# First dense pass of an attention, dense layer and routed expert kernel: work of the next block behind each step's own, five staging buffers, and expert tile 0 in another order

## The chip, the cores and the metric

The kernel runs on one core of one Trainium2 chip. The metric is the device time of one execution in microseconds (us). Before the change the median of three runs is 918.85 us (918.7 to 922.15).

## What is computed

```python
# 4 batches, 8 heads, 576 tokens, head size 64, 128 features
def phi(x):
    proj = np.einsum('bhsd,df->bhsf', x, w_phi)
    proj = proj - np.max(np.abs(proj), axis=-1, keepdims=True)
    return np.concatenate([np.exp(proj), np.exp(-proj)], axis=-1)
q_p, k_p = phi(q), phi(k)
kv, z = np.einsum('bhsf,bhsd->bhfd', k_p, v), np.sum(k_p, axis=2)
x = einsum('bhsf,bhfd->bhsd', q_p, kv) / (einsum('bhsf,bhf->bhs', q_p, z)[..., None] + 1e-06)
# x as 2304 tokens of 512
h = x @ w_in                                   # 512 x 2048
x = np.maximum(0.01 * h, h) @ w_out            # 2048 x 512
# cosine of each token to 8 expert embeddings over tau; the best expert and its softmax weight
for e in range(8):
    mask = expert_idx == e
    out[mask] = gate_w[mask, None] * (np.maximum(x[mask] @ w1[e], 0.0) @ w2[e])   # 512 x 1024 x 512
```

## The kernel before

**Tiling.** The 2304 tokens are nine blocks of 256 (`j`, 0 to 8). The attention works on four pairs of heads (`p`) and, for k and v, four batches (`b`). The dense layer's 2048 inner features are sixteen chunks (`c`); the first pass over the nine blocks uses chunks 0 to 7 and writes half sums `yp_d`, the second pass uses chunks 8 to 15, adds the half sums, and makes `ys`, the input of the router and the experts. In the second pass the blocks are worked through and the routing is done; then come the tiles of 128 gathered tokens of the experts. Expert tile 0 already begins before the last block's end.

Nearly every product of fp32 quality is made from two fp32r parts, hi and lo, as three fast matmuls (lines 344 to 346 of `mm1`, and 366 of `mm2`). Some projections of the attention are full fp32 matmuls instead, which need no split: of k where `b < K_FULL`, of q where the block is under `Q_FULL`.

**The attention.** For k, `k_load` fetches `kraw`, `k_split` makes hi and lo on ScalarE (ACT) and VectorE (DVE), `k1` projects on TensorE (PE), takes the largest absolute value and makes the two exponentials `kp`, `kn` (lines 180 and 181, ACT), `k2` multiplies with v into `kvp`, copied to `KV`. For q, `q_load` fetches `qraw`, `q1` projects (line 228 or 231), copies `pr` (line 234) and finds the largest value per token; for blocks under `QM_PE` that is done by transposing on PE (`qprT`, line 239), reducing on DVE (`qtm`, 241) and transposing back (`qmxT`, 247), for the others by a reduction over the partitions on GpSimd (POOL, line 252). `q2` subtracts it and makes the exponentials `qn`, `qp` (258, 259) and the products with `KV` (270) into `qo`; `q3` divides to `xr`, transposes it on PE (`xT`, 289) and makes `xb` hi (ACT, 293) and lo (DVE, 294), the dense layer's input. Pair `p` gives the part `k = p` of the sum over 512 in `mm1`, so the last pair is needed by every product.

**The weights.** `w_load(c)` converts two halves of 512 KB (`r`, 0 and 1) from float64: `w_fetch` issues the DMA on SyncE's queue (SP, line 307) into a staging buffer `wst` (three of them), ACT casts `top` (324), DVE puts the float together as `w` (328), ACT casts it to `W` hi (332), and POOL or, for the halves in `W_DVE`, DVE subtracts for `W` lo (333).

**The order.** The prelude (lines 430 to 448) does k of batch 0 and q of block 0, with `W0[p]` weight chunks after each pair. In block `j` each step `c` loads weights (block 0 only, up to chunk `c + W_AHEAD`), runs `mm1(j, c)`, then the step's items of the attention for block `j + 1` and of the next k batch, then `mm2(j, c - 2)`:

```python
            mm1(j, c, 200 if j == NBLK - 1 else 0)
            for it in steps[c]:
                it()
```

The order on each engine is set by the framework's scheduler, which simulates the program and puts each ready instruction by priority; `tc.issue_after(x)` keeps what is in it behind `x`. In the expert phase PE, and for the tiles in `I_ACT` ACT too, go in the order as written.

**The ends of the second pass.** `y_half_b(j)` is a generator in pieces: sums `ys` on DVE (602), a Square for the norm on ACT (605); then the eight dot products with the embeddings (613, DVE) for each half; then routing (631 onward). For blocks 7 and 8 the pieces are called from places in the expert tiles: `steps` (lines 1053 onward) maps a place (tile, position) to a piece; `ENDS` is (0, 1), `DOTS` (0, 2) and (1, 0). `first_split(3)` converts a quarter of the first expert's weights (ACT cast 900, DVE subtraction 901). In an expert tile, `up` multiplies (958 to 962) into `hps`, ACT makes `hs` (965), PE transposes it (`htp`, 972), ACT casts it to `h` hi (975), DVE subtracts for lo (976).

## Time and profile before

| what | value |
|---|---|
| median of three runs | 918.85 us (918.7 to 922.15) |
| profiled execution, its time | 917.62 us |
| span in the profile | 915.8 us |
| PE busy | 879.2 us (96%) |
| weight loads of PE busy | 754.8 us (82%) |
| DVE busy | 562.0 us (61%) |
| ACT busy | 448.8 us (49%) |
| POOL busy | 223.4 us (24%) |
| mean granted TensorE clock | 0.988 |

The span runs from the first to the last recorded instruction, and the execution's own time is 1.8 us more. A row of a timeline gives start, length, engine, line, operation, the tiles it writes and reads, and how many equal instructions it stands for; in brackets the idle time of the engine before it and what ended that. "x" counts instructions. A full fp32 matmul shows as two records, and a matmul's recorded length overlaps that of the next, so the pace is read from start to start. The clock is 1.00 where TensorE is granted its full 2.4 GHz.

### The profile page before, as it was taken

To read this page: it belongs to the slowest core of one execution; us is meant where nothing else is said; L and a number is where in the kernel's file an instruction comes from. 1 tells how busy PE (TensorE), PEld (TensorE's weight loads), DVE (VectorE), ACT (ScalarE), POOL (GpSimd) and SP (SyncE) were. 2 spreads that over 40 slices of the span, in tenths; PEclk is the share of its full clock that TensorE was granted. 3 is DMA by queue.
4 is the path that set the end of the run, shared out by engine and by line. 5 is a ranking of instruction groups with operands and counts; after the bars stand their busy time and mean duration, and the time that the engine had idled before them with its cause. 6 is when DMAs were issued, how large, how long until landed. Compare 5 with 4: busy or idle time off the path is not lost. (4 is left out here: it accounts for less than half of the span.)

```text
span 915.8 us, 18701 instructions
## 1 busy us (share of the span) xinstructions
PE 879.2 (96%) x7080; PEld 754.8 (82%) x7080; DVE 562.0 (61%) x1308; ACT 448.8 (49%) x902; POOL 223.4 (24%) x219
## 2 busy tenths in 40 slices
PE   7989999999999999899999999979999999999994
PEld 6768888889988888889888888868888788888883
DVE  6876557584856554757988889895513751113461
ACT  5965556484755544853333333442324752224571
POOL 2420113031211321032233333420112521112321
PEclk9989999999999999999999999999999999999998
DMA  8873423132221210952222222610115931115570
GB/s 290 275 227 124 134 76 120 58 122 96 58 98 36 104 65 17 337 202 96 92 94 92 93 92 93 231 46 24 36 51 186 341 120 47 48 35 181 181 264 25
DMA packets 42613, 112.36 MB, mean 123 GB/s; under 512 B 4558, under 2 KB 23118, under 8 KB 36496
## 3 DMA queue, kind: packets, MB, share of 16 engines
q1 hardware_dynamic: 33424, 61.48, 20.5%
q0 software_dynamic: 9008, 49.55, 15.5%
q8 instruction: 57, 0.93, 0.4%
q14 instruction: 44, 0.36, 0.1%
q10 hardware_dynamic: 80, 0.03, 0.0%
HBM read 87.45 MB, written 24.90 MB: 123 GB/s over the span
## 5 line engine op out<-in xcount | busy, mean ns | idle before, releaser
L366 PE MATMUL y<-W,gg 128*128 128x512 f32 x864 | 230.2, 399 | 0.6 <-POOL gg L355 0.4
L366 PEld LDWEIGHTS y<-W,gg 128*128 128x128 f32 x864 | 152.5, 189 | 28.5 <-POOL gg L355 1.0
L344 PE MATMUL h<-xb,W 128*128 128x256 f32 x576 | 163.9, 287 | 5.1 <-DVE g L351 3.2
L345 PE MATMUL h<-xb,W 128*128 128x256 f32 x576 | 162.9, 284 | 0.6 <-DVE xb L294 0.6
L346 PE MATMUL h<-xb,W 128*128 128x256 f32 x576 | 162.2, 283 | 0.0
L344 PEld LDWEIGHTS h<-xb,W 128*128 128x128 f32 x576 | 108.1, 189 | 12.7 <-DVE g L351 4.2
L613 DVE CUSTOM_DVE_ANT_0 jk<-ys,enb 128x512 f32<-128x512 f32 x144 | 114.2, 793 | 3.1 <-DVEq L913 1.1
L345 PEld LDWEIGHTS h<-xb,W 128*128 128x128 f32 x576 | 108.5, 189 | 6.5 <-DVE xb L294 1.2
L252 POOL PARTITION_ALL_REDUCE qmx<-pr x28 | 56.4, 2014 | 220.1 <-ACT pr L234 216.6
L346 PEld LDWEIGHTS h<-xb,W 128*128 128x128 f32 x576 | 108.7, 189 | 1.2
L353 ACT CAST gg<-g 128x256 fp32r<-128x256 f32 x144 | 57.6, 406 | 95.4 <-DVE g L351 88.8
L349 ACT ACTIVATE t<-h 128x256 f32<-128x256 f32 x144 | 54.6, 382 | 86.2 <-PE h L346 85.4
L351 DVE TENSOR_TENSOR g<-h,t 128x256 f32<-128x256 f32 x144 | 60.1, 420 | 51.8 <-ACT t L349 47.8
L355 POOL TENSOR_TENSOR gg<-g,gg 128x256 fp32r<-128x256 f32 x72 | 57.1, 797 | 136.2 <-ACT gg L353 118.9
L901 DVE TENSOR_TENSOR wlo<-raw,whi 128x1024 fp32r<-128x1024 f32 x56 | 67.4, 1241 | 36.7 <-ACT whi L900 34.1
L976 DVE TENSOR_TENSOR h<-htp,h 128x512 fp32r<-128x512 f32 x46 | 31.7, 689 | 82.4 <-ACTq L913 70.7
L958 PE MATMUL hps<-whi,xt 128*128 128x512 f32 x184 | 77.4, 421 | 0.7 <-DVE g L351 0.7
L988 PE MATMUL yo<-whi,h 128*128 128x512 f32 x184 | 74.5, 405 | 0.0
L959 PE MATMUL hps<-wlo,xt 128*128 128x512 f32 x184 | 73.7, 401 | 0.0
L989 PE MATMUL yo<-wlo,h 128*128 128x512 f32 x184 | 72.7, 395 | 0.0
L900 ACT CAST whi<-raw 128x1024 fp32r<-128x1024 f32 x56 | 55.9, 1046 | 28.4 <-PE hps L962 12.8
L965 ACT ACTIVATE hs<-hps 128x512 f32<-128x512 f32 x46 | 27.4, 595 | 67.3 <-PE hps L962 62.2
(233 smaller groups left out, 1595.6 us busy)
## 6 DMA issues: line engine op xcount, KB each, us to landing
wst<-in_moew_dram SPq DMA_DIRECT2D x32, 512.0 KB, 5.6
qraw<-in_q_dram SPq DMA_DIRECT2D x36, 256.0 KB, 3.1
xs_d<-xb SPq DMA_DIRECT2D x9, 1024.0 KB, 5.2
xb<-xs_d POOLq DMA_DIRECT2D x9, 1024.0 KB
kraw<-in_k_dram SPq DMA_DIRECT2D x16, 288.0 KB, 3.2
yp_d<-yt SPq DMA_DIRECT2D x9, 512.0 KB, 4.1
yt<-yp_d SPq DMA_DIRECT2D x9, 512.0 KB, 3.8
y_d<-ys SPq DMA_DIRECT2D x18, 256.0 KB, 2.1
```

The source lines that it names most:

```text
L344: nc.tensor.matmul(hp, w[:, 0, ks], x[:, 0, k, :], start=(k == 0), stop=False)
L345: nc.tensor.matmul(hp, w[:, 0, ks], x[:, 1, k, :], start=False, stop=False)
L346: marks["mm1"] = nc.tensor.matmul(hp, w[:, 1, ks], x[:, 0, k, :], start=False, stop=(k == 3))
L351: nc.vector.tensor_tensor(out=g, in0=hp, in1=t, op=ALU.max)
L353: nc.scalar.copy(out=gg[:, 0, :], in_=g)
L366: nc.tensor.matmul(yps[j][t], gg[:, a, ts], w[:, b, DM:2 * DM], start=(c0 == 0 and a == 0 and b == 0), stop=(c0 == NCH - 1 and a == 1),)
L613: nc.vector.tensor_tensor_reduce(out=jk2, in0=ys, in1=enb[:, e, :], scale=1.0, scalar=0.0, op0=ALU.mult, op1=ALU.add, accum_out=lgr[:, t, ...
L901: nc.vector.tensor_sub(lo[:, hs_], raw[c][:, hs_], hi[:, hs_].bitcast(F32))
L958: nc.tensor.matmul(ps, x[:, 0, k], hi[:, ks], start=(k == 0), stop=False)
L959: nc.tensor.matmul(ps, x[:, 0, k], lo[:, ks], start=False, stop=False)
L988: nc.tensor.matmul(yacc[i], h2[:, 0, k], hi[:, w0], start=(nh == 0 and k == 0), stop=False)
L989: nc.tensor.matmul(yacc[i], h2[:, 0, k], lo[:, w0], start=False, stop=False)
```

## The change

Constants: ten more weight halves are subtracted on DVE (6 to 15), block 1's largest values go to POOL, two more pairs of k (batch 1, pairs 2 and 3) are split into hi and lo and projected by fast matmuls, the prelude converts one chunk less, and block 0 converts two ahead and not three. `K_FULL` counts pairs now. In the first pass five staging buffers are used, three `wst` and two that take the place of `yt` tiles, and `w_ahead` fetches into them before they are converted. In block 0 each step's items are kept behind that step's last `mm1` matmul and its `t`; `k_split` of batches 1 to 3 is kept behind the last `t`. The second pass's first three fetches are kept behind the write of block 8's `xs_d`. After half 5 a small reduction on POOL is added (`warm`). In `y_half_b` the Squares come behind both sums, and for block 8 behind the break; `first_split(3)` moves from `ENDS` to the first of `DOTS`.

```diff
@@ -38,18 +38,19 @@
 BIG = 8192.0
 PRIO = 1000
 J_UP = 9
-W_DVE = tuple(range(16, 32))
+W_DVE = tuple(range(6, 32))
 N_HEAD = 3
+N_STAGE = 5
 N_TOP = 2
 K_MOD = 2
 K_SET = (1,)
-QM_PE = 2
+QM_PE = 1
 Q_FULL = 2
-K_FULL = 2
+K_FULL = 6
 G_DVE = 9
 W00 = 0
-W0 = (0, 1, 1, 2)
-W_AHEAD = 3
+W0 = (0, 1, 1, 1)
+W_AHEAD = 2
 N_FREE = 5
 P_AFTER = 2
 POS = (3, 3)
@@ -142,7 +143,7 @@
 
     def k_split(b, p):
         raw = kraw.pop((b, p))
-        if b < K_FULL:
+        if NPAIR * b + p < K_FULL:
             khl[b, p] = raw
             return
         hl = at.tile([P, 2, S], F32R, tag="khl", name="khl", bufs=2)
@@ -159,7 +160,7 @@
             ps = ps_a.tile([P, 2, 2 * F], F32, tag="pj", name="kproj")
         for i in range(n):
             s0 = min((2 * sp + i) * P, S - P)
-            if b < K_FULL:
+            if NPAIR * b + p < K_FULL:
                 nc.tensor.matmul(ps[:, i, :], hl[:, s0:s0 + P], wfull, start=True, stop=True)
                 continue
             for a, w, st in ((0, 0, True), (0, 1, False), (1, 0, False)):
@@ -294,7 +295,7 @@
             nc.vector.tensor_sub(xb[j][:, 1, p, :], ps, xb[j][:, 0, p, :].bitcast(F32)),
         )
         if p == NPAIR - 1:
-            nc.sync.dma_start(out=xs_d[j], in_=xb[j].bitcast(F32))
+            marks["xs"] = nc.sync.dma_start(out=xs_d[j], in_=xb[j].bitcast(F32))
 
 
     wc = {}
@@ -302,7 +303,10 @@
     fetched = {}
 
     def w_fetch(c, r, pool=None):
-        raw = (pool or xg).tile([P, DM + 1, 2], I32, tag="wst", name="wst", bufs=4 if pool else 3)
+        spare = not pool and c < NCH and (2 * c + r) % 5 >= N_HEAD
+        raw = (pool or xg).tile(
+            [P, DM + 1, 2], I32, tag="yt" if spare else "wst", name="wst", bufs=2 if spare else 4 if pool else 3
+        )
         halves = raw.bitcast(I16).rearrange("q n t -> q (n t)")
         nc.sync.dma_start(
             out=halves[:, 1:4 * DM + 1], in_=moew[c, :, r * DM:(r + 1) * DM].bitcast(I16)
@@ -331,7 +335,15 @@
                 )
             nc.scalar.copy(out=t[:, 0, rs], in_=w32)
             (nc.vector if (2 * c + r) in W_DVE else nc.gpsimd).tensor_sub(t[:, 1, rs], w32, t[:, 0, rs].bitcast(F32))
+            if 2 * c + r + 1 == W_DVE[0]:
+                warm = wk.tile([P, 1], F32, name="warm")
+                nc.gpsimd.partition_all_reduce(warm, t[:, 1, r * DM:r * DM + 1].bitcast(F32), P, bass_isa.ReduceOp.absmax)
         wc[c] = t
+
+    def w_ahead():
+        for n in range(2 * len(wc), min(2 * len(wc) + N_STAGE, 2 * NCH)):
+            if (n // 2, n % 2) not in fetched:
+                w_fetch(n // 2, n % 2)
 
     gs = {}
     yps = {}
@@ -346,7 +358,7 @@
             marks["mm1"] = nc.tensor.matmul(hp, w[:, 1, ks], x[:, 0, k, :], start=False, stop=(k == 3))
         with tc.high_priority(offset=ahead):
             t = xg.tile([P, BLK], F32, tag="t", name="t")
-            nc.scalar.activation(out=t, in_=hp, func=AF.Copy, scale=0.01)
+            marks["t"] = nc.scalar.activation(out=t, in_=hp, func=AF.Copy, scale=0.01)
             g = xg.tile([P, BLK], F32, tag="g", name="g")
             nc.vector.tensor_tensor(out=g, in0=hp, in1=t, op=ALU.max)
             gg = xg.tile([P, 2, BLK], F32R, tag="gg", name="gg", bufs=3)
@@ -395,7 +407,8 @@
 
         def first():
             if (b, p) not in khl:
-                k_split(b, p)
+                with tc.issue_after(marks["t"].ins) if b else nullcontext():
+                    k_split(b, p)
             if (b, p) not in vsb:
                 v_load(b, p)
             nb, np_ = (b, p + 1) if p + 1 < NPAIR else (b + 1, 0)
@@ -435,6 +448,7 @@
             it()
         for _ in range(W0[p]):
             w_load(len(wc))
+            w_ahead()
         if p == 2:
             q2(0, 0)
         if p == 3:
@@ -483,11 +497,16 @@
         for c in range(NCH):
             while j == 0 and len(wc) < min(c + W_AHEAD, NCH):
                 w_load(len(wc))
+                w_ahead()
             mm1(j, c, 200 if j == NBLK - 1 else 0)
-            for it in steps[c]:
-                it()
+            with ExitStack() as behind:
+                for m in ("mm1", "t") if j == 0 else ():
+                    behind.enter_context(tc.issue_after(marks[m].ins))
+                for it in steps[c]:
+                    it()
             if j == NBLK - 2 and c < N_HEAD:
-                w_fetch(NCH + c // 2, c % 2)
+                with tc.issue_after(marks["xs"].ins):
+                    w_fetch(NCH + c // 2, c % 2)
             if j == NBLK - 1:
                 w_load(NCH + c)
                 w_more(c + 4)
@@ -601,11 +620,16 @@
             ys = xg.tile([P, DM], F32, tag="xb" if j == NBLK - 1 else "ys", name="ys")
             nc.vector.tensor_add(ys, yps[j][t], yt[:, t, :])
             nc.sync.dma_start(out=y_d[i * P:(i + 1) * P, :], in_=ys)
+            yss.append(ys)
+        yps.pop(j)
+        if j == NBLK - 1:
+            yield
+        for t, ys in enumerate(yss):
+            i = 2 * j + t
             jk = xg.tile([P, DM], F32, tag="jk", name="jk", bufs=1)
             nc.scalar.activation(out=jk, in_=ys, func=AF.Square, accum_out=sst[:, i:i + 1])
-            yss.append(ys)
-        yps.pop(j)
-        yield
+        if j == NBLK - 2:
+            yield
         lgr = rt.tile([P, 2, NE], F32, tag="lgr", name="lgr")
         for t, ys in enumerate(yss):
             for e in range(NE):
@@ -1046,7 +1070,10 @@
         mm2(j, 2 * NCH - 1)
         xb.pop(j)
         next(ends_of[j])
+
+    def last_pair():
         first_split(3)
+        next(ends_of[j - 1])
 
     def last_route():
         next(ends_of[j], None)
@@ -1054,7 +1081,7 @@
 
     steps = {
         ENDS: ends,
-        DOTS[0]: lambda: next(ends_of[j - 1]),
+        DOTS[0]: last_pair,
         DOTS[1]: lambda: next(ends_of[j]),
         ROUTE[0]: lambda: next(ends_of[j - 1]),
         ROUTE[1]: lambda: next(ends_of[j - 1], None),
```

On PE around the block's first product `h`. Before, four transposes `qprT` and one of the full-precision projections of the next items stand between the first products:

```order
L344 MATMUL h<-xb,W 128x256
L239 MATMUL qprT<-ident,pr 128x128 x2
L289 MATMUL xT<-ident,xr 128x128 x2
L345 MATMUL h<-xb,W 128x256
L346 MATMUL h<-xb,W 128x256
L239 MATMUL qprT<-ident,pr 128x128 x2
L163 MATMUL kproj<-wfull,kraw 128x256
L289 MATMUL xT<-ident,xr 128x128 x2
L344 MATMUL h<-xb,W 128x256
L247 MATMUL qmxT<-ident,qtm 128x128 x4
```

and of the change, from the block input's last transposition `xT` on:

```order
L290 MATMUL xT<-ident,xr 128x128 x2
L356 MATMUL h<-xb,W 128x256 x2
L357 MATMUL h<-xb,W 128x256
L358 MATMUL h<-xb,W 128x256
L229 MATMUL qproj<-qraw,wfull 128x256 x2
L164 MATMUL kproj<-wfull,kraw 128x256 x2
L357 MATMUL h<-xb,W 128x256
L358 MATMUL h<-xb,W 128x256
```

The first projections of the next query block and k batch now come behind the first products, 18 of which stand ahead of this last transposition; the transposes `qprT` and `qmxT` of query block 1 are gone.

On ACT around the fourth `xb` cast. Before:

```order
L324 CAST top_100<-wst 128x512
L180 ACTIVATE kn<-kp 64x256
L181 ACTIVATE kp<-kp 64x256
L332 CAST W<-w_911 128x512
L324 CAST top_99<-wst 128x512
L258 ACTIVATE qn<-qp 128x512
L234 COPY pr<-qproj 128x512
L332 CAST W<-w_918 128x512
L259 ACTIVATE qp<-qp 128x512
L332 CAST W<-w_1047 128x512
L324 CAST top_100<-wst 128x512
L293 CAST xb<-xT 128x256
```

and of the change:

```order
L204 COPY KV<-kvp 128x260
L294 CAST xb<-xT 128x256 x3
L328 CAST top_99<-wst 128x512
L328 CAST top_100<-wst 128x512
L336 CAST W<-w_1002 128x512
L328 CAST top_99<-wst 128x512
L336 CAST W<-w_1007 128x512
L328 CAST top_100<-wst 128x512
L294 CAST xb<-xT 128x256
```

The exponentials and the copy for the next block and batch are no longer ahead of the fourth cast; weight conversions still are.

On ACT in expert tile 0. Before:

```order
L605 ACTIVATE jk,sst<-ys 128x512 x2
L900 CAST whi<-raw_5450 128x1024 x2
L975 CAST h_8175<-htp 128x512
L965 ACTIVATE hs<-hps 128x512
L913 COMPARE_AND_BRANCH
L900 CAST whi<-raw_5448 128x1024 x2
```

and of the change:

```order
L999 CAST h_8149<-htp 128x512
L924 CAST whi<-raw_5438 128x1024 x2
L630 ACTIVATE jk,sst<-ys 128x512
L989 ACTIVATE hs<-hps 128x512
L937 COMPARE_AND_BRANCH
L924 CAST whi<-raw_5436 128x1024 x2
```

The cast of `h` now stands ahead of the weight casts and the Squares, one of which is left ahead of `hs`. On DVE the subtraction for `h` lo moves to a place behind `ys` and one dot product; before, dots, routing and three of four weight subtractions stood between.

## Rows read from the trace of the kernel before

**Rows 1.** The page: busy time and share of each engine.

```profile
PE 879.2 (96%) x7080; PEld 754.8 (82%) x7080; DVE 562.0 (61%) x1308; ACT 448.8 (49%) x902; POOL 223.4 (24%) x219
```

**Rows 2.** Stretches: length; busy PE, PEld, DVE, ACT, POOL; clock; DMA share; GB/s.

```profile
0.00:48.35 48.35, 40.67 (x526) 32.26 (x527) 35.05 (x64) 36.18 (x67) 15.38 (x18) 1.00 0.85 273
48.35:67.50 19.15, 15.79 (x129) 12.46 (x126) 15.01 (x33) 13.44 (x28) 6.67 (x5) 0.82 0.74 236
67.50:80.00 12.50, 12.50 (x149) 10.77 (x147) 8.22 (x17) 6.60 (x13) 1.38 (x1) 1.00 0.63 211
...
615.00:620.00 5.00, 4.04 (x12) 3.40 (x13) 4.84 (x16) 0.58 (x1) 0.00 (x0) 0.50 0.02 3
```

**Rows 3.** Waits of PE up to 80 us: total, times, longest.

```profile
PE kproj L163 <- DMA kraw<-in_k_dram: 4.7, 1, 4.7
```

**Rows 4.** Timeline of PE, 20 to 82 us.

```profile
23.09 1.89 PE L163 MATMUL kproj<-wfull,kraw 128*128 128x256 f32 x8
...
48.35 0.39 PE L344 MATMUL h<-xb,W 128*128 128x256 f32 x1
...
77.27 0.66 PE L239 MATMUL qprT<-ident,pr 128*128 128x128 f32 x4
77.86 0.27 PE L195 MATMUL kvp<-v,kn 128*64 128x65 f32 x1
...
81.31 0.28 PE L345 MATMUL h<-xb,W 128*128 128x256 f32 x1
81.43 0.28 PE L346 MATMUL h<-xb,W 128*128 128x256 f32 x1
```

**Rows 5.** Timeline of ACT around the casts of xb.

```profile
43.06 0.61 ACT L259 ACTIVATE qp<-qp 128x512 f32<-128x512 f32 x1
...
64.90 0.36 ACT L293 CAST xb<-xT 128x256 fp32r<-128x256 f32 x1
```

**Rows 6.** Groups of ACT by line, up to 350 us: busy, mean ns, idle before.

```profile
L324 ACT CAST top<-wst 128x512 f16<-128x512 bf16 x19 | 14.5, 772 | 5.0 <-DMA wst<-in_moew_dram 4.9
L332 ACT CAST W<-w 128x512 fp32r<-128x512 f32 x16 | 9.8, 612 | 0.1
```

**Rows 7.** Single lines: ns least/median/most, first and last start.

```profile
L328 DVE SCALAR_TENSOR_TENSOR w<-wst,top x32: 681/691/1617, 14.3 to 393.7; 128x512 int32<-128x512 int32 x32
...
L333 POOL TENSOR_TENSOR W<-w,W x16: 1266/1280/1784, 17.5 to 68.6; 128x512 fp32r<-128x512 f32 x16
L333 DVE TENSOR_TENSOR W<-w,W x16: 680/684/694, 367.1 to 395.9; 128x512 fp32r<-128x512 f32 x16
...
L224 DVE TENSOR_TENSOR qst<-qraw,qst x28: 689/1200/1546, 47.0 to 338.0; 64x512 fp32r<-64x512 f32 x28
...
L252 POOL PARTITION_ALL_REDUCE qmx<-pr x28: 1939/1940/2446, 108.8 to 344.6; - x28
```

**Rows 8.** Waits of SyncE's queue up to 110 us.

```profile
SPq L307 <- DVE w L328: 23.2, 14, 2.8
```

**Rows 9.** Timeline of SyncE's queue at 55 us.

```profile
55.11 0.34 SPq L307 DMA_DIRECT2D wst<-in_moew_dram  x1
```

**Rows 10.** Timeline of PE in expert tile 0.

```profile
615.96 1.09 PE L972 MATMUL htp<-ident,hs 128*128 128x128 f32 x4 [4.83 <-DVE m L636]
```

**Rows 11.** Timeline of DVE in expert tile 0.

```profile
608.29 1.28 DVE L602 TENSOR_TENSOR ys<-y,yt 128x512 f32<-128x512 f32 x2
...
612.15 1.23 DVE L901 TENSOR_TENSOR wlo<-raw,whi 128x1024 fp32r<-128x1024 f32 x1 [0.21 <-DVEq L913]
...
615.12 0.68 DVE L976 TENSOR_TENSOR h<-htp,h 128x512 fp32r<-128x512 f32 x1
```

**Rows 12.** Timeline of ACT in expert tile 0.

```profile
610.39 1.98 ACT L900 CAST whi<-raw 128x1024 fp32r<-128x1024 f32 x2
612.27 0.57 ACT L975 CAST h<-htp 128x512 fp32r<-128x512 f32 x1
612.75 0.60 ACT L965 ACTIVATE hs<-hps 128x512 f32<-128x512 f32 x1
```

## The prediction

> **What bounds the kernel now.** I read the page first, then the table of stretches, the waits of TensorE (PE), the timelines around them, and last the groups by line. The page has PE busy for 879.2 us of a span of 915.8, so nearly the whole program is paced by PE [rows 1]: an edit counts where it takes work off PE or fills a hole in it, and work moved between the other engines counts only through these holes. The holes that the change touches are two.
>
> The first lies before 80 us [rows 2]. Up to the first matmul of the dense layer, at 48.35 us [rows 4], PE is busy for 40.67 of 48.35 us: 7.68 lost, of which 4.7 is the wait for the first k [rows 3], so 3.0 in small waits. From 48.35 to 67.5 it is busy for 15.79 of 19.15, 3.36 lost, and its granted clock is 0.82, which costs 15.79 x 0.18 = 2.8. From 67.5 it is full at clock 1.00. The end of that stretch is the fourth piece of the block's input, xb: its cast on ScalarE (ACT) starts at 64.90 [rows 5], and without it no product of the dense layer can be finished, so PE has only filler until then. What I count as lost besides the first k is 3.0 + 3.4 + 2.8 = 9.2 us.
>
> The second is in expert tile 0: PE waits 4.83 us at a transposition, htp, for VectorE (DVE) [rows 10], and runs from 615 to 620 at clock 0.50 [rows 2], busy 4.04 there, so some 2 us lost, 0.3 more around it: 4.83 + 2.3 = 7.1.
>
> The edits touch no other stretch of PE that I found waiting; the weight reload near 366 us keeps its place in ACT's and SyncE's order, and I count nothing there.
>
> **The change part by part.** The sum is made against the profiled execution, 917.62 us; the median of the runs is 918.85, so 1.2 higher (0.13%).
>
> *Block 1's max to GpSimd.* For the four head pairs of query block 1, four transposes of pr and four of the maxima go: eight groups of four. One group takes 0.59 us from its start at 77.27 to the next instruction at 77.86 [rows 4]. 8 x 0.59 = 4.7 us of PE work gone, in a stretch where PE has no hole to absorb it. In its place come four reductions of about 1.94 us on GpSimd [rows 7], which otherwise has little there; each must be through before its pair's exponentials, two steps later. Four DVE reductions go too, worth nothing by themselves. **-4.7**. Bounds: -4.7 and, if these reductions hold up the exponentials, about 0.
>
> *Two more k pairs split.* Ten full-precision projections become thirty of the faster type. The old kind shows as two records each: 1.89 us for four, 0.47 each [rows 4], 4.7 in all. The new ones pass at the pace of equal shape in the dense layer, 0.12 us from start to start (81.31 to 81.43) [rows 4]: 3.6. **-1.0**, bounds -1.0 and 0. The two extra casts and two subtractions lie in block 1, beside a PE that is behind.
>
> *The first block.* Before the first product, PE's order of before has ten full-precision projections for the next query block and k batch, 10 x 0.47 = 4.7 us, which now come behind the step's own products. So PE comes to the first product at 48.35 - 4.7 = 43.7, if the 3.0 of small waits stay. What matters is when xb is complete. On ACT, the last query exponential starts at 43.06 [rows 5]; ahead of it in the old order stand a copy and two exponentials of the next block, about 1.6 (up to 0.61 each [rows 5]), so ACT is through near 42 and copies KV by 43. Three xb casts then take 1.1, ending at 44. Ahead of the fourth cast the new order has four top casts (0.77 each [rows 6]) and two W casts (0.61 each [rows 6]), 4.3, as the old had as many and more; that makes 48.4, and with a wait for the transposition before it (xr and two transposes behind the DVE items) I take the fourth cast at **49.5**, the subtraction behind it at 50. Against 64.90 that is 15 us earlier, but PE has less to do meanwhile: 18 products at 0.12 (2.2) and output matmuls and transposes, about 1.8, fill 4.0 of the 6.3 between 43.7 and 50. So 2.3 of idle time, and I allow 1.5 more for the first chunks, where each product waits for its own t, g and gg. With half of the old clock loss (1.4, as the stretch with holes is about half as long): 3.0 + 2.3 + 1.5 + 1.4 = 8.2 instead of 9.2, **-1.0**. Bounds: with no hole left after 43.7 and full clock 3.0 (-6.2); with the fourth cast as late as 55, +4, in rival 1.
>
> The data can be there: the fetches of weight halves wait for a staging buffer freed by DVE, 23.2 us in 14 waits [rows 8]; the 14th half is asked for only at 55.11 [rows 9]. With five buffers these can be asked for earlier. By 48.35 us the DMA engines moved 273 GB/s x 48.35 = 13.2 MB at 0.85 of their share [rows 2]; sixteen halves of 0.52 MB are 8.4 MB, with k, v and q of the start 4 to 5 more. So the transfers just fit, near 47 us, without much room.
>
> Of these halves, ten subtractions move from GpSimd (1280 ns) to DVE (684 ns) [rows 7]. Four stand before the fourth transposition on DVE: 4 x 0.68 = 2.7 of added DVE time. While GpSimd works, DVE's own items stretch: w's operation takes 691 in the median and 1617 at most, and the subtraction of q 689 at least and 1200 in the median, where the reductions run [rows 7]. The Trainium skill, GPSIMD Engine Reference, section 8 (Key points), says that GpSimd shares its SBUF interfaces with VectorE and contends with its instructions that have two SBUF inputs. By that rule a GpSimd subtraction that goes gives DVE back most of what it took; the trace agrees in the sign (1617 against 681). From the rows alone: if the 2.7 is repaid by some 2.2 of stretches that go (three of 0.72, the mean of 1617 - 691 and 1200 - 689), the cast stands at 49.5; if nothing is repaid it is 2.2 later and the sum -8.2 instead of -10.4.
>
> Work pushed back in block 0 goes behind t in the queues of PE, ACT and DVE: the k splits and next projections. They are due only a block later, and PE is full from 67.5 on [rows 2], so I cost this at nothing; were that cover gone, block 1's start would wait instead, at about the size of rival 1. The second pass's first fetches move to block 7, where SyncE has little queued; nothing.
>
> *Expert tile 0.* Before, ACT has two Squares ahead of the cast of htp, which wait for the sums ys on DVE, made at 608.29 [rows 11]; so the cast stands at 612.27, behind them and two weight casts, and hs at 612.75 [rows 12]; DVE's subtraction of h, which PE waits for, starts at 615.12, behind a row of dots, routing and weight subtractions [rows 11]. Now ACT casts h first (possible from about 608, when that transposition is done), and DVE makes the subtraction right behind ys and one dot, near 610.2. Behind it come two weight casts (1.98), a Square (like hs) and hs: PE's htp near 611.9 instead of 615.96, a wait of 0.8. Then the next product needs both halves of xt, which come behind two weight subtractions on DVE, near 615.8: about 1.6 in two waits. 2.4 instead of 4.83, and the low clock halved (1.0 for 2.3): **-3.7**. Bounds: -6.3 (both waits gone) and 0.
>
> Sum: -4.7 - 1.0 - 1.0 - 3.7 = -10.4; 917.62 - 10.4 = **907.2 us**, about 908.4 on the footing of the median.
>
> **The rivals.**
> (1) *The hole in block 0 moves and doesn't shrink.* DVE gets four subtractions more, and with the W conversions they delay the cast to about 55. Then 11.3 - 4.0 = 7.3 from 43.7 is idle, and 3.0 + 7.3 + 1.5 + 1.4 = 13.2 is lost, +4.0 against the 9.2 of before in place of -1.0. 917.62 - 4.7 - 1.0 + 4 - 3.7 = 912.2. For it: ACT and DVE are busy for 36 and 35 of the 48 us [rows 2]. Against: they lose work of the next block there. Chance 0.2.
> (2) *Slower.* The conversions now stand in order ahead of the fourth cast, so if half 14 still lands late (asked for at 55 as in [rows 9], or the DMA engines are held up by five fetches at once), the cast stays near 65 and PE, with its filler now behind t, stands for 18.3, from 43.7 + 4.0 to 66: 3.0 + 18.3 + 1.5 + 1.4 = 24.2 lost, +15.0 against 9.2, with -9.4 from the rest: 917.62 + 5.6 = 923.2, or 926.9 where expert tile 0 gains nothing. It decides, against no change, when the cast comes after about 60 (from 49.5, each us later costs one, until the 10.4 are used up). Against it: the buffers that made these fetches wait are five now. Chance 0.06.
> (3) *Expert tile 0 gains nothing*: the wait goes from htp to xt's low half, because DVE's weight subtractions (1.2 us each) stand before it either way. 907.2 + 3.7 = 910.9. Chance 0.12.
> (4) *Better*: the clock doesn't fall in block 0 and the hole there is 3 us, expert tile 0 gains all of 6.3: 907.2 - 4 - 2.6 = 900.6. Chance 0.1.
>
> **How the numbers follow.** The forecast has 0.52. The range, 899 to 916, takes in the bounds of block 0 for the forecast (902 to 912), rivals 1, 3 and 4, and leaves out rival 2 and mixtures of 1 and 3 with more. No change is within 0.5%, 4.6 us, about what a measurement of this kernel can tell: 914.3 to 923.4 against the median. Faster: forecast, rival 4, and most of 1 and 3, 0.79; same: the rest of these and half of rival 2, 0.14; slower 0.07.
>
> **What would show it.** Right: PE's first product near 44, the fourth xb cast near 50, PE full from about 52; before 80 us eight groups of transposes fewer; htp of expert tile 0 waits about 1 us, the stretch 615 to 620 (shifted) at more than half clock. Wrong: the fourth cast after 55, SyncE still waiting for staging buffers after 40, PE waiting in block 1 for reductions, or the wait in expert tile 0 as long at xt as it was at htp.

## The result and the profile after

The changed kernel takes **906.09 us** (median of 4 runs, 905.77 to 907.3) against 918.78 before; the ratio is 0.9874, 95% interval [0.9846, 0.9902]. Forecast were 907.2, with 899 to 916. In a second session (the run c1_after_again below) it took 907.68, ratio 0.9875 [0.9852, 0.9898]. The total was right within 1.1 us (2.3 on the footing of the median, 908.4). Its parts were not: the first pass gave 2.4 of the 6.7 us forecast for it, and gains that were not forecast made up for it. One run of experiment 9, 966.19 us at a mean granted clock of 0.846, is left out of all figures.

The profiled execution has a span of 904.3 us against 915.8. The page's first line answers to [rows 1], and the table of stretches to [rows 2] (columns as there; the row 52 to 58 is used further down):

```profile
PE 869.0 (96%) x7058; PEld 749.6 (83%) x7058; DVE 562.8 (62%) x1316; ACT 450.0 (50%) x904; POOL 218.9 (24%) x214
```

```profile
0.00:48.35 48.35, 39.59 (x560) 32.58 (x560) 37.03 (x73) 36.14 (x67) 10.93 (x15) 1.00 0.85 284
48.35:67.50 19.15, 16.38 (x117) 13.48 (x116) 16.55 (x29) 14.25 (x31) 6.48 (x3) 1.00 0.42 138
67.50:80.00 12.50, 11.88 (x162) 10.42 (x161) 8.59 (x20) 7.68 (x18) 1.94 (x1) 1.00 0.30 91
...
100.00:350.00 250.00, 245.81 (x2851) 219.21 (x2850) 155.11 (x329) 151.38 (x328) 54.29 (x28) 1.00 0.29 93
...
370.00:380.00 10.00, 10.00 (x56) 9.13 (x56) 6.73 (x15) 7.02 (x16) 0.00 (x0) 0.83 0.94 343
...
52.00:58.00 6.00, 5.83 (x32) 4.81 (x32) 6.00 (x9) 4.06 (x9) 3.63 (x2) 1.00 0.78 263
```

Three things stand in these rows. The clock does not fall between 48 and 67.5 in this execution. PE is idle for 4.2 us between 100 and 350, where it was idle for 2.8 in the kernel before. And the clock now falls between 370 and 380. The same two stretches of the kernel before, which did not stand among its rows yet:

```profile
100.00:350.00 250.00, 247.20 (x2861) 220.40 (x2860) 155.27 (x326) 149.33 (x327) 56.40 (x28) 1.00 0.27 87
...
370.00:380.00 10.00, 7.39 (x50) 6.65 (x49) 6.06 (x13) 6.12 (x14) 0.00 (x0) 1.00 0.99 345
```

The fourth xb cast on ACT (timeline), against a forecast of 49.5:

```profile
49.70 0.77 ACT L328 CAST top<-wst 128x512 f16<-128x512 bf16 x1
50.34 0.35 ACT L294 CAST xb<-xT 128x256 fp32r<-128x256 f32 x1
```

The cast at 64.90 in [rows 5], which the prediction takes for the fourth of the kernel before, is the fifth: block 1's first, behind the first `t` and `gg` of block 0. Block 0's fourth, at the end of the order that is shown under The change, stands earlier (timeline of the kernel before):

```profile
60.18 0.37 ACT L293 CAST xb<-xT 128x256 fp32r<-128x256 f32 x1 [0.41 <-PE xT L289]
```

So the change brings this cast forward by 9.8 us, not by 15.

PE in expert tile 0 (timeline, only the rows with a wait), against [rows 10]:

```profile
607.42 0.66 PE L996 MATMUL htp<-ident,hs 128*128 128x128 f32 x4 [0.48 <-ACTq L937]
...
611.32 0.96 PE L986 MATMUL hps<-whi,xt 128*128 128x512 f32 x3 [1.08 <-DVE xt L888]
```

**Where the time went, by four milestones.** Rows that mean the same work in both kernels cut the span into stretches: the first sums ys of the second pass and the last (timeline of DVE), the second cast of h in tile 0 and the last of the program (timeline of ACT). Of the kernel before (608.29 stands in [rows 11]):

```profile
419.99 1.29 DVE L602 TENSOR_TENSOR ys<-y,yt 128x512 f32<-128x512 f32 x2 [0.31 <-PE y L366]
```

```profile
617.08 0.58 ACT L975 CAST h<-htp 128x512 fp32r<-128x512 f32 x1 [3.04 <-PE htp L972]
...
898.87 0.57 ACT L975 CAST h<-htp 128x512 fp32r<-128x512 f32 x1
```

and of the changed kernel:

```profile
417.57 1.29 DVE L621 TENSOR_TENSOR ys<-y,yt 128x512 f32<-128x512 f32 x2 [0.32 <-PE y L378]
...
604.20 1.28 DVE L621 TENSOR_TENSOR ys<-y,yt 128x512 f32<-128x512 f32 x2
```

```profile
608.59 0.58 ACT L999 CAST h<-htp 128x512 fp32r<-128x512 f32 x1
...
887.55 0.57 ACT L999 CAST h<-htp 128x512 fp32r<-128x512 f32 x1
```

| stretch | before | changed | changed, second session | difference | forecast |
|---|---|---|---|---|---|
| start to the first sums | 419.99 | 417.57 | 417.18 | -2.4, -2.8 | -6.7 |
| to the last sums | 188.30 | 186.63 | 188.42 | -1.7, +0.1 | 0 |
| to the second cast of h | 8.79 | 4.39 | 4.40 | -4.4 | -3.7 with the clock behind it |
| to the last cast of h | 281.79 | 278.96 | 278.75 | -2.8, -3.0 | 0 |
| to the end of the span | 16.93 | 16.75 | 16.65 | -0.2, -0.3 | 0 |

The sums are -11.5 and -10.4. (Second session: rows 417.18, 605.60, 610.00 and 888.75, span 905.4.)

The first stretch by PE's busy time, and its end by itself, from block 7's half sums (copied at 368.34 before, 364.49 in the changed kernel) to the first sums. Before:

```profile
0.00:419.99 419.99, 403.10 (x4385) 353.39 (x4386) 261.60 (x560) 253.88 (x541) 90.31 (x76) 0.99 0.42 136
368.34:419.99 51.65, 48.60 (x312) 43.55 (x311) 30.14 (x80) 31.37 (x68) 9.63 (x23) 1.00 0.70 245
```

and of the changed kernel:

```profile
0.00:417.57 417.57, 397.49 (x4363) 350.31 (x4364) 262.65 (x568) 254.83 (x543) 84.13 (x71) 1.00 0.41 136
364.49:417.57 53.08, 49.34 (x310) 44.46 (x309) 30.38 (x80) 30.96 (x69) 9.63 (x23) 0.97 0.67 235
```

PE is busy for 5.6 us less and idle for 3.2 us more (20.1 for 16.9). Of the added idle time 1.1 lies before 80 us (12.15 for 11.04), 1.4 between 100 and 350, and 0.7 behind block 7's half sums. That last part, with two matmuls fewer on record, is 1.4 us longer as a whole, and 1.1 in the second session (52.72).

### The profile page after: what moved, and what is told of

Read it like the earlier page. It is cut to its first block, busy times and chain, and to the rows that moved or that the text cites. A ratio compares the mean times of both kernels' runs of the same rounds, so it can differ in the third digit from the quotient of the medians.

```text
span 904.3 us, 18660 instructions
## 1 busy us (share of the span) xinstructions
PE 869.0 (96%) x7058; PEld 749.6 (83%) x7058; DVE 562.8 (62%) x1316; ACT 450.0 (50%) x904; POOL 218.9 (24%) x214
## 5 line engine op out<-in xcount | busy, mean ns | idle before, releaser
L253 POOL PARTITION_ALL_REDUCE qmx<-pr x32 | 62.7, 1965 | 246.5 <-ACT pr L235 203.9
```

Of the source, the lines that this page charges most:

```text
L253: nc.gpsimd.partition_all_reduce(mx.rearrange("q h t -> q (h t)"), pr.rearrange("q h t -> q (h t)"), P, bass_isa.ReduceOp.absmax)
```

## The experiments

The theory after the result: PE's work and its holes set the time. 5.7 us of PE work went, block 0 lost less, tile 0 gained 4.4, and the wait near 366 with the small waits of the first pass gave a part of it back. The rivals are in each expectation. The kernel before ran beside each group: 919.54, 918.51 and 919.33 in the three sessions.

**1. Block 1's largest values on PE again.**

```diff
-QM_PE = 1
+QM_PE = 2
```

> The change, with block 1's largest values taken by transposes on PE again (QM_PE 2). Theory (PE full, so its work counts in full): 32 transposes come back, 8 x 0.59 = 4.7 us, so 910 to 911.5. Rival (the reductions on GpSimd cost as much by waits as they save): within 1 us of 906.1. Second rival: the transposes delay the first block too, over 912.

Measured: 916.24 us (915.45 to 917.88, 11 runs), ratio to before 0.9967 [0.9953, 0.9981]. That is 8.6 to 10.2 us over the changed kernel's two medians, about twice the theory's 4.7. The second rival's figure came in, and its mechanism in part: the fourth cast stands at 50.30 as in the changed kernel, but the loss does arise in the first two blocks. Block 0's half sums are copied at 101.05 (89.86 in the changed kernel), block 1's at 140.82 (132.42), and the first sums are 8.25 later:

```profile
425.82 1.29 DVE L621 TENSOR_TENSOR ys<-y,yt 128x512 f32<-128x512 f32 x2 [0.31 <-PE y L378]
```

The stretch 48.35 to 67.5 shows where the rest is:

```profile
48.35:67.50 19.15, 16.64 (x107) 13.81 (x108) 14.79 (x29) 13.63 (x27) 0.00 (x0) 0.82 0.35 122
```

The clock is back at 0.82, 16.64 x 0.18 = 3.0 us by estimate; with 4.7 of work that is 7.7 of 8.25, and PE's idle time up to 100 us, 1.0 more, covers the rest. Whether the fall belongs to the edit is not shown: experiment 2's profile has it too, with the transposes gone, and so has experiment 11's, whose program is the changed kernel's up to 336 us (see the last section). All eleven runs here have a mean granted clock of 0.987 to 0.990, the changed kernel's nine 0.988 to 0.993, and among those nine the time does not follow it (905.77 us at 0.989, 907.3 at 0.992).

**2. All of batch 1's k by full matmuls again.**

```diff
-K_FULL = 6
+K_FULL = 8
```

> The change, with all of batch 1's k projected by full matmuls again (K_FULL 8 pairs). Theory: 10 x 0.47 for 30 x 0.12, so 1.0 us more PE work, 907 near; the casts and subtractions that go (two each on ACT and DVE) were hidden. Rival (the split items cost DVE and ACT time that PE waits for): 905 or less.

Measured: 910.52 us (909.88 to 911.47), ratio 0.9905 [0.9887, 0.9924]. Slower by 2.8 to 4.4 where 1.0 was expected. In its profile, PE's order is the changed kernel's until block 1, and yet the stretch 52 to 58 differs:

```profile
52.00:58.00 6.00, 6.00 (x17) 5.01 (x17) 5.61 (x10) 3.63 (x8) 1.96 (x1) 0.50 0.60 221
```

The clock is at its lower level, 17 matmuls are done in 6 us and not 32. Block 0's half sums are copied 1.15 us later there (91.01 against 89.86), before any work that the edit touches. That part is not the edit's. With the edit's own 1.0 and a wait for a khl cast in block 1 (0.86 at 140.88) it comes to 3.0, where the first sums are 2.6 us later. One of its runs with a mean clock of 0.994 took 909.88, those with 0.987 took 910.09 to 910.96, so the fall looks like no large part of the total, on one run of the other kind. How much of the 2.8 to 4.4 is the edit's stays open.

**3. The issue order undone: block 0's items, and the k splits of batches 1 to 3.**

```diff
-                for m in ("mm1", "t") if j == 0 else ():
+                for m in ():
...
-                with tc.issue_after(marks["t"].ins) if b else nullcontext():
+                with nullcontext():
```

> The change without the issue order in block 0: a step's items no longer stand behind its mm1 and t, and k_split not behind t; everything else as in the change. Theory: this order is what puts the fourth xb cast at 50; without it the cast comes at 55 to 65 and the clock falls again near 60, 1.7 us or more lost before 80 us: 907.5 to 909. Rival (the five buffers and the DVE subtractions alone did it): cast still before 53 and a time within 0.7 us of 906.1.

Measured: 910.26 us (909.56 to 910.96), ratio 0.99 [0.9882, 0.9918]; the fourth cast came at 59.69:

```profile
58.02 0.62 ACT L259 ACTIVATE qn<-qp 128x512 f32<-128x512 f32 x1
...
59.69 0.36 ACT L294 CAST xb<-xT 128x256 fp32r<-128x256 f32 x1
```

An exponential of the next block stands ahead of it again, and the cast is back near the 60.18 of the kernel before. The theory holds for the cast; the time is over its 907.5 to 909. The order brings the cast forward by 9.35 us, of which 2.3 arrive at the first sums (419.88); the likely reason is that without it PE does the next block's work in the meantime.

**4. The ends of the second pass as before.**

```diff
         yps.pop(j)
-        if j == NBLK - 1:
-            yield
-        for t, ys in enumerate(yss):
...
-    def last_pair():
         first_split(3)
-        next(ends_of[j - 1])
```

> The change with the ends of the second pass as before (Squares behind each sum and ahead of the break, first_split(3) back at the place of the sums). Theory: the wait at htp of 4.8 us and the half clock behind it come back: between the two casts of h in tile 0 4 to 5 us more, 910.5 to 912. Rival (the forecast's low bound: the wait only moves to xt): under 908.

Measured: 913.31 us (912.67 to 916.01), ratio 0.994 [0.992, 0.9961], 5.6 to 7.2 us slower. The wait is back, and the matmuls behind it start 0.43 apart where 0.23 is usual:

```profile
613.70 1.09 PE L991 MATMUL htp<-ident,hs 128*128 128x128 f32 x4 [4.91 <-DVE m L655]
...
615.01 0.63 PE L978 MATMUL hps<-wlo,xt 128*128 128x512 f32 x1
615.44 0.63 PE L977 MATMUL hps<-whi,xt 128*128 128x512 f32 x1
```

From the last sums to the second cast of h it takes 8.79 us (606.03 to 614.82) as before the change. The mechanism held; the time is over the expected 910.5 to 912. Of the 5.6 us by which this profile's span (911.0) is above the second session's of the changed kernel (905.4), 4.4 lie here.

**5. The kernel before with these ends alone.**

```diff
+        if j == NBLK - 1:
+            yield
...
-        DOTS[0]: lambda: next(ends_of[j - 1]),
+        DOTS[0]: last_pair,
```

> The kernel before, with only the ends of the second pass in the change's order. Theory: tile 0's wait of 4.8 us at htp becomes waits of 0.5 and 1.1, and the half clock behind it goes; 4.4 us and about 1 of clock: 5 to 6 us under the kernel before of the same chip. Rival (the gain needs the rest of the change, or goes to another wait): under 2 us.

Measured: 914.06 us (911.8 to 917.34, 10 runs), ratio 0.9958 [0.9935, 0.998], 4.5 us faster where 5 to 6 were expected; 4.43 us from the last sums to the second cast (607.44 to 611.87). This part stands by itself.

**6. Ten subtractions back on GpSimd.**

```diff
-W_DVE = tuple(range(6, 32))
+W_DVE = tuple(range(16, 32))
...
-            if 2 * c + r + 1 == W_DVE[0]:
+            if 2 * c + r == 5:
```

> The change, with ten weight-lo subtractions (halves 6 to 15) back on GpSimd; the small reduction stays behind half 5. Theory from the rows (four subtractions of 0.68 us leave DVE ahead of the fourth xb cast, some 2.2 us of stretched DVE items come back): cast within 1 us of 50.3, time within 1 us of 906.1, or 908 with the 2 us of the stretch 553 to 609 that the other variants showed. Rival (the subtractions on DVE were the gain, since GpSimd's slowed DVE down): cast after 52, w's operation at up to 1.6 us again, 909 or more. Rival on the other side (DVE is what the cast waits for): cast before 49.

Measured: 934.77 us (932.83 to 935.69), ratio 1.0177 [1.0133, 1.0222]: 27 to 29 us slower than the changed kernel. The signs of the first rival came in (fourth cast at 63.16, w's operation at up to 1754 ns, over 909), but the size is not explained by its mechanism. The timeline of GpSimd tells where it comes from:

```profile
35.69 0.41 POOL L340 PARTITION_ALL_REDUCE warm<-W  x1 [5.89 <-issue]
45.41 5.38 POOL L337 TENSOR_TENSOR W<-w,W 128x512 fp32r<-128x512 f32 x4 [9.31 <-issue]
...
75.74 1.96 POOL L253 PARTITION_ALL_REDUCE qmx<-pr  x1 [6.18 <-issue]
84.83 1.28 POOL L337 TENSOR_TENSOR W<-w,W 128x512 fp32r<-128x512 f32 x1 [7.14 <-issue]
92.27 3.90 POOL L253 PARTITION_ALL_REDUCE qmx<-pr  x2 [6.16 <-issue]
```

Each turn from subtractions to reductions costs 5.9 to 6.2 us in which GpSimd waits for nothing that the profile shows, and each turn back 7.1 to 9.3. The Trainium skill, GPSIMD Engine Reference, section 2.1 (Instruction dispatch), says that the first call of a freshly loaded GpSimd kernel takes about 6 us more, with no instruction in the profile for it. The trace agrees for the reductions and shows more for the way back. DVE waits for GpSimd, 10.72 us at 46.69 for a subtraction and 10.89 at 94.26 for a reduction, and PE for DVE (timeline of PE):

```profile
50.27 1.11 PE L248 MATMUL qmxT<-ident,qtm 128*128 128x128 f32 x4 [10.85 <-DVE qtm L242]
...
97.35 1.62 PE L164 MATMUL kproj<-wfull,kraw 128*128 128x256 f32 x3 [11.24 <-DVE kp L178]
```

Up to 110 us there are five turns here and one in the changed kernel. The first two are the small reduction's, which this variant keeps behind half 5 with subtractions still to come: PE's first wait lies behind them, the second behind the turns around block 1's reductions. So with the ten subtractions left on GpSimd, these reductions cost more by this wait than they save. How much of the 27 to 29 us goes without the small reduction was not run.

**7. All three edits of GpSimd's work undone.**

```diff
-W_DVE = tuple(range(6, 32))
+W_DVE = tuple(range(16, 32))
-QM_PE = 1
+QM_PE = 2
...
-            if 2 * c + r + 1 == W_DVE[0]:
-                warm = wk.tile([P, 1], F32, name="warm")
```

> The change without its three edits of GpSimd's work: subtractions of halves 6 to 15 on GpSimd, block 1's largest values on PE, no small reduction. To be held against the run with the largest values on PE alone (916.2). Theory (the subtractions matter only where reductions stand between them, by GpSimd's idle 6 to 9 us at each turn from one to the other): fourth xb cast within 1.5 us of 50.3, time 914.5 to 917.5. Rival (subtractions on GpSimd slow DVE down, or are late themselves): cast after 52, 918 or more.

Measured: 916.41 us (914.43 to 916.99, 10 runs), ratio 0.9963 [0.995, 0.9976], beside 0.9967 in experiment 1; the fourth cast at 51.28. Held: where no reduction stands between, the time is the same with the ten subtractions on either engine. That is a trade and not the absence of a cost. w's operation on DVE takes 692 ns in the median here and 691 in experiment 1, but the median hides those that meet a subtraction on GpSimd. Four of these, and the subtractions beside them (timelines of DVE and GpSimd):

```profile
50.35 2.82 DVE L332 SCALAR_TENSOR_TENSOR w<-wst,top 128x512 int32<-128x512 int32 x2 [0.20 <-ACT top L328]
...
53.43 3.10 DVE L332 SCALAR_TENSOR_TENSOR w<-wst,top 128x512 int32<-128x512 int32 x2
```

```profile
49.67 9.23 POOL L337 TENSOR_TENSOR W<-w,W 128x512 fp32r<-128x512 f32 x6 [9.54 <-ACT W L336]
```

and one in experiment 1, where GpSimd has none:

```profile
50.78 0.69 DVE L332 SCALAR_TENSOR_TENSOR w<-wst,top 128x512 int32<-128x512 int32 x1
```

Of the 32 here, eight take 1.14 to 1.75 us, and each of them starts while a subtraction runs on GpSimd; in experiment 1 there are three such, beside the subtractions of the first six halves, and all others take at most 0.70 in both. The eight are longer by 5.9 us in all, the three by 1.9. So the subtractions on GpSimd cost DVE some 4 us, and on DVE they cost 10 x 0.68 = 6.8.

**8. Without the small reduction.**

```diff
-            if 2 * c + r + 1 == W_DVE[0]:
-                warm = wk.tile([P, 1], F32, name="warm")
-                nc.gpsimd.partition_all_reduce(warm, ...
```

> The change without the small reduction behind half 5. Theory (the first reduction after other work pays some 6 us on GpSimd, and the small one paid them early): block 1's first reduction ends at 62 to 65 and not 58, its exponentials wait, 907 to 911. Rival (GpSimd is set up for reductions as soon as its last subtraction is done, at 30, long ahead of the first at 54.4): first reduction at 54 to 55, within 1 us of the changed kernel.

Measured: 906.78 us (905.67 to 907.71), ratio 0.9864 [0.9837, 0.9892]. The rival was right. The view of the reduction's line has a row of GpSimd's queue, with the first and last start of the set-up, right after the last subtraction; the timeline has the first reduction on time:

```profile
L253 POOLq MODIFY_POOL_CONFIG  x2: 18/18/18, 29.2 to 29.3; - x2
```

```profile
54.17 4.12 POOL L253 PARTITION_ALL_REDUCE qmx<-pr  x2 [24.87 <-ACT pr L235]
```

A gap of 25 us without work hides the 6. The small reduction is worth nothing measurable here.

**9. Three staging buffers, no early fetch.**

```diff
-        spare = not pool and c < NCH and (2 * c + r) % 5 >= N_HEAD
+        spare = False
...
-            if (n // 2, n % 2) not in fetched:
-                w_fetch(n // 2, n % 2)
+            pass
```

> The change with three staging buffers and no early fetch. Theory (the fetches' waits for a buffer are what makes the last halves late): half 14 asked for after 44, the fourth cast at 54 to 60, 3 us or more slower than the change: 909 to 914. Rival (conversion, not the transfer, sets the pace): cast before 52 and a time within 1 us, or 908 with the stretch 553 to 609.

Measured: 913.83 us in the median of nine runs (912.5 to 915.43), ratio 0.9956 [0.9933, 0.9978]. The fetches of the first block's last halves are issued at 39.39 and from 51.29, where the changed kernel issues its last at 48.02; the fourth cast waits for its transposition and comes at 53.56:

```profile
53.56 0.37 ACT L294 CAST xb<-xT 128x256 fp32r<-128x256 f32 x1 [0.51 <-PE xT L290]
```

The first sums come at 422.34, 4.8 us later. The time is as the theory has it, the cast just ahead of its 54 to 60. The path is not shown: PE's idle time up to 80 us is 11.8 and not more than the changed kernel's 12.15, while the clock is 0.93 up to 48.35 and 0.91 from there to 67.5 (by estimate 39.20 x 0.07 + 16.73 x 0.09 = 4.2). Block 0's half sums come 4.3 later (94.14 for 89.86). Whether the late fetches or the execution lowered the clock is open. Another 2 us lie behind tile 0, see the last section.

**10. The changed kernel again.**

> The changed kernel itself, beside the next three on the same chip. 905.8 to 907.3 as measured; over 909 would mean that the differences of 2 us between the variants in the stretch 553 to 609 come with the execution and not with the kernel.

Measured: 907.68 us (907.15 to 908.99). Its profile has the same milestones within 0.4 us up to 553, and then takes 1.8 us more to the last sums. The place is a DVE instruction that starts without a wait in the first session (576.58) and 2.82 us late here (timeline of DVE):

```profile
579.19 0.16 DVE L836 TENSOR_SCALAR egi<-pp 128x5 int32<-128x5 f32 x1 [2.82 <-PE h L358]
```

The kernel before has 2.74 there, experiments 1 to 4 2.88 to 2.98, at a time when the experts' first weights come in. All four profiles of experiments 5, 6, 9 and 11, which were run in one session, start it without a wait, among them experiment 5's, of the kernel before with other ends, whose second stretch is 186.73. So the -1.7 of the second stretch goes with the execution or the session, not with the change. What the instruction waits for stays open.

**11. The last block's weight conversions behind t.** The wait near 366 is 3.74 us in the changed kernel (3.24 in the second session) and 2.61 before. PE's rows, before and changed:

```profile
373.05 0.39 PE L344 MATMUL h<-xb,W 128*128 128x256 f32 x1 [2.61 <-DVE g L351]
```

```profile
369.79 0.39 PE L356 MATMUL h<-xb,W 128*128 128x256 f32 x1 [3.74 <-DVE g L363]
```

Rows of ACT there, in the changed kernel:

```profile
364.49 1.08 ACT L387 COPY yt<-y 128x512 f32<-128x512 f32 x2
367.92 0.76 ACT L328 CAST top<-wst 128x512 f16<-128x512 bf16 x1 [2.35 <-DMA wst<-in_moew_dram]
368.55 0.64 ACT L361 ACTIVATE t<-h 128x256 f32<-128x256 f32 x2
```

Two t, whose products PE had finished by 366, stand behind a weight cast that waits for its DMA.

```diff
-                w_load(NCH + c)
+                with tc.issue_after(marks["t"].ins):
+                    w_load(NCH + c)
```

> The change, and in the last block of the first pass each chunk's weight conversion of the second pass is issued behind that step's t (three lines). Theory: the wait of 3.7 us near 366 (PE on g, g on t, t behind a weight cast on ACT that waits for its DMA) goes, with the lower clock behind it (0.83 from 370 to 380): 3 to 5 us faster, 901 to 903. Rival (the weights then come late, and PE waits for them at the second pass's first products): within 1 us of 906, with the wait at W.

Measured: **903.64 us** (903.07 to 905.61), ratio 0.9841 [0.98, 0.9882], the lowest median of all kernels here, just above the expected 901 to 903, and 2.5 to 4 us under the changed one. All four of its runs are under the changed kernel's fastest (905.77), though the intervals of the two ratios overlap. The wait shrinks to 0.52 and the clock stays at 1.00:

```profile
368.06 0.39 PE L356 MATMUL h<-xb,W 128*128 128x256 f32 x1 [0.52 <-DVE g L363]
```

```profile
370.00:380.00 10.00, 8.35 (x54) 7.14 (x54) 8.58 (x18) 7.73 (x17) 0.00 (x0) 1.00 0.99 375
```

A wait of 1.6 at the second product (for gg, on ACT) takes some of it back. From block 7's half sums to the first sums it is 50.55 us (365.46 to 416.01), with eight matmuls fewer, for 53.08 and 52.72 in the changed kernel and 51.65 before.

**12. The same with all k from batch 1 on split.**

```diff
-K_FULL = 6
+K_FULL = 4
```

> The change with the last block's weight conversions behind t (903.6 alone) and K_FULL 4, so that all k from batch 1 on are split. Theory: 10 full matmuls at 0.47 for 30 at 0.12, 1.0 us less PE work: 902.5. Rival (two more casts and subtractions in block 1 make PE wait): 904 or more.

Measured: 906.8 us, spread over 904.72 to 911.04 (6 runs), ratio 0.9871 [0.9844, 0.9897]. By its profile the first sums come at 414.05, 2 us before experiment 11's, but the time does not show it: it is the rival's figure (904 or more), without its mechanism in that profile. Not settled; K_FULL stays at 6.

## Why the prediction was right, and where it was not

*Block 1's max to GpSimd, -4.7.* Right in kind, larger in size when undone alone: 8 to 10 us, up to 3.0 of them through the clock between 48 and 67.5. The bound "about 0, if the reductions hold up the exponentials" did not come in. What the forecast left out is the condition: the subtractions must leave GpSimd first (experiments 6 and 7). It costed that move as a trade of 2.7 us against 2.2 on DVE; experiment 7 shows a trade of that kind, some 4 us for the 6.8 of all ten, with no difference in the time. The 27 to 29 us where the two sorts of work alternate were not in the forecast.

*K pairs, -1.0.* The work is as counted (x80 records of full projections become x60, x120 fast ones x150). The time of experiment 2 is larger, perhaps in part by the clock.

*The first block, -1.0.* The new cast was forecast rightly, 50.34 for 49.5; the old one was misread, 64.90 for 60.18. The loss of 9.2 does not rest on that row, the words of rival 2 (the cast stays near 65) do. Lost in the changed kernel, besides the first k: 8.76 - 4.7 = 4.1 before 48.35, then 2.8 and 0.6, and nothing through the clock: 7.5 against 9.2, so -1.7 by the forecast's own sum. The idle time was 7.5 where 6.8 was forecast and 6.4 stood before: it grew, and the whole gain is the clock, which does not hold in every execution. In experiment 11's profile the clock falls here as before, 16.89 x 0.18 = 3.0 by estimate; idle time is 1.3 less, and block 0's half sums come 1.45 later (91.31). "Each us later costs one" was too dear: in experiment 3 a cast 9.35 later costs 2.6 to 4.2 us of time.

*Expert tile 0, -3.7.* -4.4, and some 0.5 of clock behind it (7.14 us for 7.69 from the second to the third cast of h). Waits of 0.5 and 1.1 for 0.8 and 1.6; rival 3, xt as the new place, is there as one of these 1.1 us.

*The step that failed* is "the weight reload near 366 us keeps its place in ACT's and SyncE's order, and I count nothing there". Its order stayed, its wait did not: 3.74 for 2.61, and then a clock of 0.83 from 370 to 380. From block 7's half sums to the first sums, a stretch that holds both, it is 1.4 us longer (1.1 in the second session) where 0 was forecast. With it failed "the edits touch no other stretch of PE that I found waiting": small waits between 100 and 350 grew by 1.4. The sum for the first pass was -5.7 of work, -1.4 of clock and +0.4 of idle time, -6.7; measured are -5.6 busy and +3.2 idle, -2.4. Of the 4.3 that are missing, 2.8 are idle time; the other 1.5 are PE's busy time, in which the new low clock near 370 and an overrated clock at the start are not told apart. A wait that depends on when a transfer lands can change when the work ahead of it becomes shorter. Experiment 11, which changes the order there, takes 2.5 to 4 us off.

*What made the sum right* is in good part luck. Against the forecast the first pass gave 4.3 too little; tile 0 gave 0.7 more, the second stretch 1.7, which other executions do not have, the stretch behind tile 0 2.8, of which 0.5 is the clock and the rest was not foreseen, and the end 0.2. Rival 1 (cast at 55) and rival 2 did not occur, rival 4 only in its clock. Experiment 3 has rival 1's case, with the cast even later, and costs 2.6 to 4.2 where rival 1's price is 5 (912.2 against 907.2).

*The edits do not add up.* Undone one at a time, the five of experiments 1, 2, 3, 4 and 9 cost 8.6 to 10.2, 2.8 to 4.4, 2.6 to 4.2, 5.6 to 7.2 and 6.2 to 7.7 us, 26 to 34 together, and the whole change gave 11.7 to 12.7. These figures say what each is worth beside the others, and are no shares of the gain.

## What to carry to other kernels

When work is taken off a full engine, list the places later on where it waits for a DMA or a slower queue: these can absorb a part of the gain unless the order there is changed too, as the three lines of experiment 11 do. Check that a row is the one that is meant by counting from the start: the fifth cast was taken for the fourth here. On GpSimd, count the turns between kinds of work before counting instructions. Compare two profiles by rows that mean the same work; a right total hid wrong parts here. Do not read what an edit costs when undone as its share of the whole.

## What was not expected of the hardware

GpSimd's turns between elementwise work and reductions, 5.9 to 9.3 us each where nothing hides them.

How plainly DVE and GpSimd get in each other's way: w's operation takes 0.69 us, and 1.14 to 1.75 where it starts while a GpSimd subtraction runs (experiment 7). Where the subtraction is the one that starts second, it is longer instead: 1.50 and 1.74 us for 1.27, beside two w of 0.69 that started before it.

A steady difference of matmul pace in the expert phase. Means between 660 and 880 us by line (busy, mean ns), of the three-buffer kernel of experiment 9:

```profile
L985 PE MATMUL hps<-whi,xt 128*128 128x512 f32 x140 | 38.3, 395 | 0.0
```

and of the changed kernel, the same line of code:

```profile
L986 PE MATMUL hps<-whi,xt 128*128 128x512 f32 x140 | 37.6, 391 | 0.0
```

From the second to the last cast of h the three kernels with three staging buffers (before, experiments 5 and 9) take 281.8, 281.7 and 281.0 us, and the eleven profiles of kernels with five 278.5 to 279.5. The staging buffers are not used in that phase, so where the later tiles come to lie may be the cause; that was not tried.

The clock after the same short hole: between 52 and 58 us it is 1.00 in both profiles of the changed kernel and 0.50 in that of experiment 2, with the same order of PE up to there and nearly the same waits before it (1.23, 0.48 and 0.65 us against 1.23, 0.49 and 0.63). Experiment 11's program is the changed kernel's up to 336 us, and its profile has the fall too:

```profile
52.00:58.00 6.00, 5.65 (x15) 4.73 (x16) 5.60 (x10) 4.02 (x9) 1.96 (x1) 0.50 0.61 221
```

Whether it falls there differs between executions.
